# Seven-product form for the first two batches' outputs, queries of batch 2 transposed on TensorE, and tail stores by quarter block

## The chip, the cores and the metric

One core of one Trainium2 chip. The time is that of the whole kernel on the device, in microseconds (us), median of its runs. The traces give a span, first to last instruction, which is some 1.8 us shorter. In the profile PE is TensorE's matmuls, PEld its weight loads, DVE VectorE, ACT ScalarE, POOL GpSimd, SP SyncE. A line such as `67.48 0.50 PE L293 ... [1.83 <-DVE t_bkv L271]` is: start, duration, engine, source line, operation, output and input, and in brackets the engine's idle time just before it and what ended it.

## The reference

Eight batches of 8 heads, 576 tokens and 64 channels go through an attention over 32 memory slots, then a SwiGLU block with 512 channels and a hidden width of 1536. The kernel takes and gives float32, and computes in bfloat16.

```python
a = softmax over tokens of phi                     # phi: 8 x 8 x 576 x 32
k_m = einsum('bhsm,bhsd->bhmd', a, k); v_m = the same with v
attn = softmax(q @ k_m.T / sqrt(64)) @ v_m         # 8 x 8 x 576 x 64
x = attn.transpose(0, 2, 1, 3).reshape(4608, 512)
g = x @ w_gate; val = x @ w_val                    # 512 -> 1536
out = (g * sigmoid(g) * val) @ w_out               # 1536 -> 512
```

## The kernel before

The kernel runs batches 0 and 1 together, up to about 54 us, then a batch at a time. Output products of a batch wait in a `backlog` and are fed to TensorE between the steps of the next one.

For batches 2 to 7 the product with `w_out` is made of seven products of half blocks instead of eight (a Winograd form). It needs block sums of the hidden activations (`t_S`: four operations for each of three chunks, two of the chunks on GpSimd and one on VectorE) and of the weights (`t_T`: four for each chunk, once, on VectorE). Batches 0 and 1 take the plain product, which needs no sums:

```python
def out_units(b, u, eng):          # plain: 12 matmuls of 512 columns for 128 tokens
    ...
        nc.tensor.matmul(mine["p"], lhsT=hts[b, jf // 4][:, jf % 4, 128 * u:128 * (u + 1)],
                         rhs=WO[jf], start=(jf == 0), stop=(jf == NJF - 1))
    ...
def weight_sums(c):                # VectorE, both inputs in SBUF
    ...
    subtract(v, t[:, 0], B12, B11);  subtract(v, t[:, 1], B22, t[:, 0])
    subtract(v, t[:, 2], B22, B12);  subtract(v, t[:, 3], B21, t[:, 1])
    Ts[c] = t
def chunk_done(b, c):              # when chunk c of batch b's hidden activations is complete
    ...
    if b < FAST:                   # FAST = 2: no sums for batches 0 and 1
        ends()
        return
    eng = nc.vector if c + 1 == NCH else nc.gpsimd
    ...
    eng.tensor_tensor(out=t[:, 0], in0=A21, in1=A22, op=ALU.add)
    subtract(eng, t[:, 1], t[:, 0], A11)
    subtract(eng, t[:, 2], A11, A21)
    subtract(eng, t[:, 3], A12, t[:, 1])
    ...
```

Each product takes a bank of PSUM, from a list of eight in the order in which they were given back. A product is summed in its bank, VectorE adds it to a stored earlier one, and the bank is free. In the list of seven, "s", "a" and "c" are banks, and several products go to the same one:

```python
first = product("s", A(0, 0), W_(0, lo), "p1") + product("a", A(1, 0), W_(1, lo), "c11")
five = product("c", Sx(0), T(0), "p5")
six = product("s", Sx(1), T(1), "q6")
three = product("c", Sx(3), W_(1, hi), "c12")
seven = product("s", Sx(2), T(2), "c22")
four = product("s", A(1, 1), T(3), "c21")
return first + five + six + three + seven + four, ops
```

`p1`, `p5`, `q6` are ScalarE's copies of a bank; `c11` to `c21` are the additions that complete an output quarter (VectorE). Queries of batches 2 and 3 share one buffer (`Q_SLOT = (0, 1, 0, 0, ...)`); those of batch 2 are transposed by the DMA.

The softmax here doesn't subtract the row's maximum and nothing guards it: scores larger than these inputs give would overflow.

## Time and profile before

| | before |
|---|---|
| time, median (first runs: lowest to highest) | 238.47 us (238.07 to 242.48) |
| span of the profiled execution, granted clock | 237.7 us, 0.998 |
| PE busy | 225.7 us (95%) |
| batch 2's first scores, batch 3's first scores (first matmul of L400) | 67.03, 96.89 us |
| PE waits between 54 and 100 us | 1.7 for `t_qT`, 0.5 small |
| from PE's last matmul to the end | 5.1 us |

The two rows of scores are the marks to go by: between them and after them the work is the same, so a change shows as a shift of the marks.

### The profile page before, as it was taken

The page shows a single profiled execution, that of the slowest core. Times are in us where ns is not written, and L with a number is a line of the kernel's source. Part 1 is how long each engine was busy: PE and PEld are TensorE (multiplying, and loading weights), DVE is VectorE, ACT ScalarE, POOL GpSimd, SP SyncE. Part 2 cuts the span into 40 slices and gives each one's busy share as a digit, 9 for nine tenths or more (in the row PEclk, how much of TensorE's full clock was granted, in tenths as well). Part 3 has the DMA queues.
Part 4 walks back from the last instruction along what each step waited for, and adds up shares of the span by engine and source line. Part 5 has one row for each costly group of instructions (what it writes and reads, how often), then busy time and mean ns, then how long its engine had stood idle before and what let it go on. Part 6 is the DMA issues. An engine that isn't in the chain of part 4 may idle for free.

```text
span 237.7 us, 7051 instructions
## 1 busy us (share of the span) xinstructions
PE 225.7 (95%) x2745; PEld 163.0 (69%) x2751; DVE 183.0 (77%) x410; ACT 169.5 (71%) x361; POOL 110.5 (47%) x149
## 2 busy tenths in 40 slices
PE   7988899999999999799999999999999999999991
PEld 2554467775544767587778777877788778878880
DVE  4247699995578888698789878988799879987621
ACT  2768889986067769687898779968897788677310
POOL 8523432000072297344992499167926492039400
PEclk9999999999999999999999999999999999999999
DMA  6999999998889999999169954999396621122206
GB/s 212 204 205 206 199 207 209 242 235 182 112 176 208 254 190 95 203 242 209 47 120 201 256 110 99 201 290 121 94 167 145 116 89 24 39 53 88 47 8 190
DMA packets 44592, 37.41 MB, mean 157 GB/s; under 512 B 17680, under 2 KB 39696, under 8 KB 44560
## 3 DMA queue, kind: packets, MB, share of 16 engines
q0 software_dynamic: 21424, 22.42, 56.2%
q1 hardware_dynamic: 22160, 13.38, 26.5%
q10 hardware_dynamic: 976, 1.18, 1.5%
q8 instruction: 21, 0.34, 0.6%
q14 instruction: 11, 0.09, 0.2%
HBM read 42.47 MB, written 9.44 MB: 218 GB/s over the span
## 4 chain that ended last, share of the span: by engine, by line
PE 65%; DMA 20%; DVE 7%; ACT 2%; issue 2%; POOL 2%; DVEq 0%; POOLq 0%
PE p_g L514 16%; PE p_v L514 15%; PE p_os L713 9%; PE p_oo L633 8%; DMA t_qT<-t_q 8%; DMA W<-in_moe_w_gate_dram 7%; PE p_u L471 4%; PE p_oc L713 4%; DMA t_kv<-in_k_dram 3%; PE p_oo L661 3%; PE p_oa L713 2%; DMA t_kT<-t_bkv 2%; ACT t_U L491 2%; PE p_kv L235 2%; DVE t_lz L443 1%
## 5 line engine op out<-in xcount | busy, mean ns | idle before, releaser
L537 DVE TENSOR_TENSOR t_h<-t_sg,p_v 128x288 bf16<-128x288 bf16 x192 | 83.7, 452 | 14.9 <-PE p_v L514 9.6
L514 PEld LDWEIGHTS <-t_U 128*128 128x128 bf16 x768 | 73.8, 98 | 22.2 <-issue 2.6
L531 ACT ACTIVATE t_sg<-p_g 128x288 bf16<-128x288 f32 x192 | 75.1, 420 | 18.8 <-PE p_g L514 11.8
L514 PE MATMUL p_g<-t_A,t_U 128*128 128x288 bf16 x384 | 77.1, 286 | 0.1
L514 PE MATMUL p_v<-t_A,t_U 128*128 128x288 bf16 x384 | 76.9, 286 | 0.0
L491 ACT CAST t_U<-p_u 128x512 bf16<-128x512 f32 x53 | 28.0, 607 | 8.4 <-PE p_u L471 8.4
L713 PEld LDWEIGHTS <-t_S 128*128 128x128 bf16 x288 | 28.2, 98 | 3.3
L598 POOL TENSOR_TENSOR t_S<-t_h 128x512 bf16<-128x512 bf16 x12 | 13.9, 1154 | 35.6 <-DVE t_h L537 35.6
L713 PEld LDWEIGHTS <-t_h 128*128 128x128 bf16 x216 | 20.4, 98 | 6.2 <-issue 3.2
L633 PE MATMUL p_oo<-WO,t_h 128*128 128x512 bf16 x90 | 21.6, 379 | 0.6 <-issue 0.5
L115 POOL DMA_DIRECT2D t_q<-in_q_dram x6 | 4.8, 798 | 32.2 <-DMA t_qT<-t_q 30.7
L713 PE MATMUL p_os<-t_T,t_S 128*128 128x256 bf16 x144 | 17.7, 273 | 0.0
L633 PEld LDWEIGHTS <-t_h 128*128 128x128 bf16 x96 | 9.0, 98 | 10.6 <-issue 1.1
L471 PE MATMUL p_u<-W,t_kT 64*32 64x512 bf16 (+1 forms) x416 | 16.0, 363 | 0.3 <-DMA W<-in_moe_w_gate_dram 0.2
L661 PE MATMUL p_oo<-WO,t_x 128*128 128x256 bf16 x96 | 14.5, 273 | 0.0
L560 POOL TENSOR_TENSOR t_S<-t_S,t_h 128x512 bf16<-128x512 bf16 x12 | 13.8, 1154 | 0.9
L560 POOL TENSOR_TENSOR t_S<-t_h,t_S 128x512 bf16<-128x512 bf16 x12 | 13.9, 1155 | 0.0
L560 POOL TENSOR_TENSOR t_S<-t_h 128x512 bf16<-128x512 bf16 x12 | 13.9, 1155 | 0.0
L836 PE MATMUL p_warm<-bones 128*128 128x512 bf16 (+2 forms) x43 | 12.1, 406 | 1.7 <-DVE bones L859 1.7
L495 DVE CAST t_U<-p_u 128x512 bf16<-128x512 f32 x19 | 12.4, 683 | 1.5 <-PE p_u L471 1.5
L451 DVE TENSOR_TENSOR t_A<-t_E,t_lz 128x576 bf16<-128x576 bf16 x16 | 12.1, 757 | 1.2 <-DVE t_lz L443 0.5
L411 ACT ACTIVATE t_E<-p_g 128x288 bf16<-128x288 f32 x12 | 5.0, 414 | 10.4 <-PE p_v L400 10.4
(93 smaller groups left out, 311.5 us busy)
## 6 DMA issues: line engine op xcount, KB each, us to landing
t_kv<-in_k_dram POOLq DMA_DIRECT2D x8, 576.0 KB, 8.1
t_kv<-in_v_dram POOLq DMA_DIRECT2D x8, 576.0 KB, 14.1
out_dram<-t_o SPq DMA_DIRECT2D x23, 192.0 KB, 2.9
t_phi<-in_phi_dram POOLq DMA_DIRECT2D x6, 576.0 KB, 16.3
t_q<-in_q_dram POOLq DMA_DIRECT2D x6, 576.0 KB, 10.8
out_dram<-t_o SPq DMA_DIRECT2D x36, 64.0 KB, 2.6
out_dram<-t_o SPq DMA_DIRECT2D x15, 128.0 KB, 3.8
WO<-in_moe_w_out_dram POOLq DMA_DIRECT2D x3, 512.0 KB, 18.8
```

The source lines that it names most:

```text
L451: nc.vector.tensor_tensor(out=a, in0=es.pop((b, g)), in1=lzs.pop((b, g)), op=ALU.mult)
L471: nc.tensor.matmul(p[g][32 * i:32 * i + 32, o:o + n], lhsT=kTs[b][64 * g:64 * g + 64, 2, 32 * i:32 * i + 32], rhs=w_part(w, c, i, g, halve ...
L491: nc.scalar.copy(out=t, in_=p)
L495: nc.vector.tensor_copy(out=t, in_=p)
L514: nc.tensor.matmul(p[:, 0:HALF], lhsT=Us[b, c, g][:, o // 2, which, 128 * (o % 2):128 * (o % 2 + 1)], rhs=atts[b, g][:, r], start=(g == 0) ...
L531: nc.scalar.activation(out=sg, in_=gate[:, 0:HALF], func=AF.Silu)
L537: nc.vector.tensor_tensor(out=dst, in0=sg, in1=val[:, 0:HALF], op=ALU.mult)
L560: eng.tensor_tensor(out=out, in0=x, in1=y, op=ALU.subtract)
L598: eng.tensor_tensor(out=t[:, 0], in0=A21, in1=A22, op=ALU.add)
L633: nc.tensor.matmul(mine["p"], lhsT=hts[b, jf // 4][:, jf % 4, 128 * u:128 * (u + 1)], rhs=WO[jf], start=(jf == 0), stop=(jf == NJF - 1),)
L661: nc.tensor.matmul(mine["p"], lhsT=xs[pair][:, jf].rearrange("p a t -> p (a t)"), rhs=WO[jf][:, cols], start=(jf == 0), stop=(jf == NJF - 1),)
L713: nc.tensor.matmul(mine[home][:, u], lhsT=lhs(c, m, u), rhs=rhs(c, m), start=fresh and u == 0, stop=(k == 5), skip_group_check=u == 1 or n ...
```

## The change

The intent: TensorE is full, so take matmul time from it (the seven-product form for batches 0 and 1 too), let batch 3's queries be loaded early, and send the last outputs sooner. The diff, cut to its core:

```diff
-    Q_SLOT = (0, 1, 0, 0, 1, 0, 1, 0)
+    Q_SLOT = (0, 1, 0, 1, 0, 1, 0, 1)
@@ chunk_done
-        if b < FAST:
-            ends()
-            return
...
+        if b == 0 and c > 0:
+            late.append(lambda: sums(nc.vector if end else nc.gpsimd))
+        else:
+            sums(nc.vector if end else nc.gpsimd)
...
+        if (b, c) in beside_sums:
+            beside_sums[b, c]()       # loads of batch 3, behind GpSimd's sums
@@ c11, c22, c12, c21
+            if box.get("end"):
+                both("o1", 0, lo)     # store a quarter as soon as it is summed
@@ start
-    load_q(2)
-    load_q(3)
+    for g in range(NG):
+        load_q_group(2, g)
@@ batch 2
-    backlog = out_list(0) + out_list(1) + out_rest(0, 0)
+    backlog = []
...
-            load_qT(2)
             phi_exp(2)
-            run(take(16))
-            weight_sums(0)
-            run(take(12))
-            run(kv_items(2)[:1] + take(6) + kv_items(2)[1:] + take(7))
-            weight_sums(1)
-            run(take(11))
+            (one, ops1), (zero, ops0) = products(1, ()), products(0, ())
+            kv, q2 = kv_items(2), q_items(2, "aava")
+            run(one[:6])
+            for c in range(NCH):
+                weight_sums(c)
+            run(one[6:12] + zero[:6] + kv[:1] + q2[:2])
+            run(one[12:18] + kv[1:] + q2[2:])
+            mark = ...                # GpSimd waits here for batch 2's keys
+            run_late()                # sums of batch 0's chunks 1 (GpSimd) and 2 (VectorE)
+            run(one[18:36])
+            backlog = zero[6:] + one[36:] + out_rest(0, 0)
...
-                ([lambda: load_qT(3)], 12, 12),
@@ end
+    box["end"] = True
     run(take(6))
     ops["c11"]()
-    box["end"] = True
```

Batch 3's query transpose is issued right after batch 2's scores instead.

More of the change, by code (lines that the diff above doesn't have):

```diff
@@ L480, in u_round @@
                 if (b, c, g) not in Us:
-                    Us[b, c, g] = upool.tile([128, 2, 2, HC], BF16, tag=f"U{c}{g}", name="t_U")
+                    u_buffer(b, c, f"U{c}")
                 if len(which) == 1:
@@ L548, in gv_slot, with u_buffer @@
         flush_mul(n)
-    def u_buffers(b):
-        for c in range(NCH):
-            t = upool.tile([128, NG, 2, 2, HC], BF16, tag=f"S{c}", name="t_U")
-            for g in range(NG):
-                Us[b, c, g] = t[:, g]
+    def u_buffer(b, c, tag):
+        t = upool.tile([128, NG, 2, 2, HC], BF16, tag=tag, name="t_U")
+        for g in range(NG):
+            Us[b, c, g] = t[:, g]
     xs, Ss, late = {}, {}, []
@@ L589, in ends, with sums @@
             )
-        if b < FAST:
-            ends()
-            return
-        eng = nc.vector if c + 1 == NCH else nc.gpsimd
-        t = upool.tile([128, 4, 2, 256], BF16, tag=f"S{c}", name="t_S")
+        t = upool.tile([128, 4, 2, 256], BF16, tag=f"U{c}" if b == 1 else f"S{c}", name="t_S")
         Ss[b, c] = t
         A11, A12, A21, A22 = blocks(b, c)
-        eng.tensor_tensor(out=t[:, 0], in0=A21, in1=A22, op=ALU.add)
-        subtract(eng, t[:, 1], t[:, 0], A11)
-        subtract(eng, t[:, 2], A11, A21)
-        subtract(eng, t[:, 3], A12, t[:, 1])
-        if c + 1 < NCH:
-            ends()
-        else:
-            late.append(ends)
+        def sums(eng):
+            eng.tensor_tensor(out=t[:, 0], in0=A21, in1=A22, op=ALU.add)
+            subtract(eng, t[:, 1], t[:, 0], A11)
+            subtract(eng, t[:, 2], A11, A21)
+            subtract(eng, t[:, 3], A12, t[:, 1])
+        end = c + 1 == NCH
+        if b == 0 and c > 0:
+            late.append(lambda: sums(nc.vector if end else nc.gpsimd))
+        else:
+            sums(nc.vector if end else nc.gpsimd)
+        if end and b > 1:
+            late.append(ends)
+        else:
+            ends()
+        if (b, c) in beside_sums:
+            beside_sums[b, c]()
+    beside_sums = {
+        (0, 0): lambda: load_q(3), (1, 0): lambda: load_k(3), (1, 1): lambda: load_v(3)
+    }
     def token_segments(b, t0, count):
@@ L623, in store @@
             eng.dma_start(out=out_r[bb, jj, pp:pp + m, cols], in_=t_o[row + r0:row + r0 + m])
-    def out_units(b, u, eng):
-        mine = {}
-        def unit(jf):
-            def run():
-                if jf == 0:
-                    mine["p"] = bank([128, DM], FP32, "p_oo")
-                nc.tensor.matmul(
-                    mine["p"],
-                    lhsT=hts[b, jf // 4][:, jf % 4, 128 * u:128 * (u + 1)],
-                    rhs=WO[jf],
-                    start=(jf == 0),
-                    stop=(jf == NJF - 1),
-                )
-                if jf == NJF - 1:
-                    t_o = work.tile([128, DM], FP32, tag="to", name="t_o")
-                    copy(eng, t_o, mine["p"])
-                    done(mine["p"])
-                    store(t_o, b, 128 * u, 128)
-            return run
-        return [unit(jf) for jf in range(NJF)]
     def out_rest(pair, half):
@@ L743, in add, with both @@
                 done(mine[home])
+        def both(name, t0, cols):
+            for u in range(2):
+                store(mine[name][:, u, cols], b, t0 + 128 * u, 128, cols=cols)
         def c11():
@@ L751, in c22 @@
             add(t[:, :, hi], "s", "p5")
+            if box.get("end"):
+                both("o2", 256, hi)
         def c12():
@@ L755, in c12 @@
             add(t[:, :, hi], "c", "q6", True)
-            for u in range(2):
-                store(t[:, u], b, 128 * u, 128)
+            both("o1", 0, hi if box.get("end") else slice(0, DM))
         def c21():
@@ L762, in c21 @@
             done(mine["s"])
-            for u in range(2):
-                store(t[:, u], b, 256 + 128 * u, 128)
+            both("o2", 256, lo if box.get("end") else slice(0, DM))
         ops = dict(
@@ L779, in products @@
         return first + five + six + three + seven + four, ops
-    FAST = 2
-    def out_list(b):
-        res = []
-        for u in range(4):
-            res += out_units(b, u, "a" if u < 2 else "v")
-        return res
     def q_items(b, evac):
@@ L880 @@
     load_phi(3, nc.gpsimd)
-    load_q(2)
-    load_q(3)
-    u_buffers(1)
+    for g in range(NG):
+        load_q_group(2, g)
+    for c in range(NCH):
+        u_buffer(1, c, f"S{c}")
     warm(104)
@@ L947, in take @@
         return part
-    KV = {b: 7 for b in range(3, B - 1)}
+    KV = 7
     def loads(b):
@@ L969 @@
         if b == 2:
-            load_qT(2)
             phi_exp(2)
-            run(take(16))
-            weight_sums(0)
-            run(take(12))
-            run(kv_items(2)[:1] + take(6) + kv_items(2)[1:] + take(7))
-            weight_sums(1)
-            run(take(11))
+            (one, ops1), (zero, ops0) = products(1, ()), products(0, ())
+            kv, q2 = kv_items(2), q_items(2, "aava")
+            run(one[:6])
+            for c in range(NCH):
+                weight_sums(c)
+            run(one[6:12] + zero[:6] + kv[:1] + q2[:2])
+            run(one[12:18] + kv[1:] + q2[2:])
+            mark = att.tile([1, 1], BF16, tag="mark", bufs=1, name="t_mark")
+            nc.gpsimd.tensor_copy(out=mark, in_=kTs[2][0:1, 0, 0:1])
+            run_late()
+            run(one[18:36])
+            backlog = zero[6:] + one[36:] + out_rest(0, 0)
         else:
@@ L980 @@
             run(take(6))
-            loads(b)
+        loads(b)
         for g in range(NG):
@@ L987 @@
         if b == 2:
-            load_k(3)
-            load_v(3)
-            load_q(4)
-            load_phi(4, nc.gpsimd)
-        else:
-            run(take(6))
+            load_qT(3)
+        run(take(6))
         z_inv_v(b, 0)
@@ L997 @@
             ops["c11"]()
-            run(take(6))
+        run(take(6))
         if not last:
@@ L1002 @@
         norm(b, 1)
-        if b > 2:
-            run(take(6))
+        run(take(6))
         run_late()
@@ L1007 @@
         if b == 2:
-            run(take(24))
+            run(take(6))
             u_three(2)
-            weight_sums(2)
         run(take(12))
@@ L1014 @@
         outs = [lambda: run(take(1)) for _ in range(len(backlog) - beside)]
-        streams = [(g, 0, 24), (outs, 4 if b > 2 else 0, 24)]
+        streams = [(g, 0, 24), (outs, 4, 24)]
         if last:
             streams += [([u_item(b, 2)], 5, 6)]
-        if b == 2:
-            streams += [
-                ([lambda: load_qT(3)], 12, 12),
-                ([lambda: (load_k(4), load_v(4))], 12, 12),
-                (kv_items(3, lambda: (u_item(2, 2, "aava")(), run(take(2)))), 12, 16),
-                ([lambda: (run(take(2)), u_three(3), run(take(3)))], 17, 18),
-            ]
-        elif not last:
-            load_qT(b + 1)
-            phi_sum(b + 1)
-            streams += [
-                (kv_items(b + 1, lambda: (u_item(b, 2, "aava")(), run(take(2)))), KV[b], KV[b] + 4),
+        if not last:
+            if b == 2:
+                streams += [([lambda: (load_k(4), load_v(4))], 12, 12)]
+            else:
+                load_qT(b + 1)
+                phi_sum(b + 1)
+            streams += [
+                (kv_items(b + 1, lambda: (u_item(b, 2, "aava")(), run(take(2)))), KV, KV + 4),
                 ([lambda: (run(take(2)), u_three(b + 1), run(take(3)))], 19, 20),
```

## The prediction

> **What bounds the kernel now.** I read the page's first two parts, then the windows by stage, the timelines of PE, POOL, DVE and the DMA queue, and the chain of waits.
>
> ```profile
> PE 225.7 (95%) x2745; PEld 163.0 (69%) x2751; DVE 183.0 (77%) x410; ACT 169.5 (71%) x361; POOL 110.5 (47%) x149
> ```
>
> PE is busy for 95% of the span, so time leaves this kernel only if PE gets less work, if one of its few holes closes, or if the ends shorten. The windows say where the holes are (length, then busy time of PE, PEld, DVE, ACT, POOL, then clock, DMA share, GB/s):
>
> ```profile
> 54.40:67.00 12.60, 12.39 (x136) 6.03 (x136) 5.91 (x18) 3.77 (x5) 0.00 (x0) 1.00 0.82 143
> 67.00:97.00 30.00, 27.89 (x341) 17.96 (x352) 25.08 (x54) 22.21 (x47) 17.11 (x23) 1.00 1.23 178
> 97.00:122.20 25.20, 25.20 (x338) 19.91 (x338) 21.05 (x45) 20.88 (x45) 16.48 (x22) 1.00 0.78 171
> 232.60:237.70 5.10, 0.00 (x0) 0.00 (x0) 0.42 (x1) 0.00 (x0) 0.00 (x0) 0.92 0.57 175
> ```
>
> A later batch takes 25.2 us and PE fills all of it. Batch 2 (54.4 to 97.0) leaves PE idle 2.3 us, and after PE's last matmul 5.1 us go to the final stores. The one large hole, with its cause:
>
> ```profile
> 40.00 0.79 POOL L115 DMA_DIRECT2D t_q<-in_q_dram  x1 [1.52 <-DMA W<-in_moe_w_val_dram]
> 67.06 0.77 POOL L115 DMA_DIRECT2D t_q<-in_q_dram  x1 [26.27 <-DMA t_qT<-t_q]
> ...
> 77.79 8.71 SPq L121 DMA_TRANSPOSE t_qT<-t_q  x1
> ...
> 96.89 0.28 PE L400 MATMUL p_g<-t_qT,t_kT 64*32 64x288 bf16 x1 [1.67 <-DMA t_qT<-t_q]
> ```
>
> Queries of batches 2 and 3 share one buffer. So POOL sits 26.3 us until the DMA transpose of batch 2 has read it, batch 3's queries are loaded late, their transpose is issued at 77.8 among the other loads and takes 19.1 us to land, and PE waits 1.67 us for it.
>
> The cost of the output products, from the chain (start, length):
>
> ```profile
> 63.22 3.88 PE p_oo L633 x18
> ...
> 102.89 1.31 PE p_os L713 x12
> ```
>
> An old 512-column matmul is 3.88/18 = 0.2156 us; a 256-column one of the seven-product form is 1.31/12 = 0.109 us. (The page counts 90 of the 96 old ones, so some records are missing and I use counts from the code.)
>
> **What the Trainium skill says.** (1) "TensorE: Matmul & The Clock Gate", section "Wait — 56ns, not 53.3ns?": a warm matmul costs N/2.4 GHz plus about 2.5 ns, so 215.8 ns for 512 columns and 109.2 for 256; the two durations above agree. (2) "VectorE: DVE Perf Modes", section "The three transpose paths": a DMA transpose is several times slower than TensorE's, whose result lands in PSUM and needs a copy. This trace agrees: 6.4 to 19.1 us to landing for a DMA transpose of one batch's queries, while 12 of the start's TensorE transposes pass in about 0.5 us (11.89 to 12.39) and a copy takes 0.45 us. (3) "GPSIMD Engine Reference", section "1. Specifications": the SBUF interface is shared with VectorE, with contention for DVE instructions that have two SBUF inputs. The trace shows it faintly: a POOL copy that lasts 0.40 us lasts 0.66 beside DVE's block sums at 197.7, and DVE's sums last 0.50 to 0.51 instead of 0.42 beside POOL's copies at 221.5. DVE's gate products at L537 (one SBUF input) stay at 0.42 to 0.45 us with or without POOL's sums. (4) "DMA: Bandwidth & Descriptors", section "Anatomy of one DMA — SWDGE (gpsimd) path": a transfer has a fixed cost of about 2 us, mostly the write receipt. A lone late store here (at 223.8) lands in 1.9 to 2.2 us.
>
> **The change part by part.**
>
> *PE work.* Removed: 96 matmuls of 512 columns, 96 x 0.2156 = 20.7 us. Added: 2 batches x 7 products x 12 matmuls = 168 x 0.109 = 18.35 us. Net -2.35 us, all on the path because PE is full here. Added: 24 transposes of batch 2's queries, 2 x 0.5 = +1.0 us. Net -1.35 us.
>
> *The hole.* With slots that alternate and batch 2's queries transposed on TensorE, batch 3's load no longer waits for a DMA transpose. It follows the first POOL sums, near 48 us; its transpose is issued right after batch 2's scores (near 68) and even with 19 us to landing is done 6 us before it is needed. -1.67 us.
> Sum if nothing new waits: -3.0. Adding up PE's new sequence from 54.6 by the same durations puts batch 3's scores at 93.4 instead of 96.89, which is -3.5 (the small holes of the old sequence go too). I take -3.2.
>
> *The new wait.* The old stage opened with about 48 matmuls that needed nothing from DVE. The new one needs, at once, all weight sums and the block sums of batch 1. DVE in program order after its last gate product at 55.2:
>
> ```profile
> 55.20 0.42 DVE L560 TENSOR_TENSOR t_T<-WO 128x512 bf16<-128x512 bf16 x1
> 55.65 0.42 DVE L560 TENSOR_TENSOR t_T<-WO,t_T 128x512 bf16<-128x512 bf16 x1
> 55.99 0.42 DVE L560 TENSOR_TENSOR t_T<-WO 128x512 bf16<-128x512 bf16 x1
> 56.33 0.42 DVE L560 TENSOR_TENSOR t_T<-WO,t_T 128x512 bf16<-128x512 bf16 x1
> ...
> 61.83 0.99 DVE L271 TENSOR_SCALAR t_bkv<-p_kv,t_rS 128x128 bf16<-128x128 f32 x4
> ```
>
> Four such operations pass in 1.45 us. There are 4 groups (block sums of the last chunk, three of weights): 5.8 us to 61.0; an output sum 0.65, a reciprocal 0.2, the four scalings 0.99: 62.8. PE's independent work from 54.6: three products 3.93, the key and value sums 0.95, 12 transposes 0.5, the first sum product 1.31: 61.3. The next thing on PE is the transpose of those scalings. So PE waits about 1.6 us at best. POOL, by its queue (second query load at 42.3 when an earlier load frees its place, then 4 x 1.15 us for each chunk's sums, copies and loads between), does the sums of batch 1's middle chunk from about 55 to 59.5, beside those very DVE operations, both with two SBUF inputs. Either DVE stretches (12 x 0.08 = 1.0 us) or POOL is held and its sums come late. I add 0.6. Wait: +2.2 us.
>
> *The tail.* DMA share by microsecond (the last columns):
>
> ```profile
> 232.00:233.00 1.00, 0.58 (x6) 0.28 (x3) 0.38 (x2) 0.00 (x0) 0.00 (x0) 1.00 0.90 285
> 233.00:234.00 1.00, 0.00 (x0) 0.00 (x0) 0.05 (x1) 0.00 (x0) 0.00 (x0) 1.00 0.96 285
> 235.00:236.00 1.00, 0.00 (x0) 0.00 (x0) 0.00 (x0) 0.00 (x0) 0.00 (x0) 1.00 0.64 223
> ```
>
> Two blocks of 512 KB and the last 128 KB, 1.15 MB, at 285 GB/s are 4.1 us, which is the stretch from 231.6 to 235.7: the tail is a transfer, not one latency. Storing each quarter when it is summed moves 512 KB ahead of 230.7. The rest then ends near 234.7, and the last store lands in about 2.1 us instead of 3.1. -1.0 us. PE's work before it does not change.
>
> *Sum.* -3.2 + 2.2 - 1.0 = -2.0 us, thus 238.47 - 2.0 = 236.5. From batch 3 on nothing moves, 25.2 us a batch.
>
> **The rivals.** (A) DVE and POOL take the whole gain of batch 2: if POOL's sums of the middle chunk cannot run at all beside DVE's chain, they end near 65.5, three products wait for them in turn, and the stall is 3 to 4 us. For it: the copy at 0.66 us above. Against: POOL may be ahead of my count. It makes 237.5 to 238.3. (B) PE's wait is covered, because POOL's and DVE's sums run faster than I count: the full 3.2 + 1.0, thus 234.3. For it: the order of the new stage puts a batch 0 product and query transposes before the first sum product. Against: the same DVE rows, which add to 62.8 without any contention. (C) POOL's sums in the stage of batches 0 and 1 slow DVE's gate products, where DVE is busy 27.1 of 28.9 us, and DVE becomes that stage's bound: 10% slower would be 29.8, +0.9 us and 237.4. Against: those products do not stretch beside POOL in later batches. (D) The quarter stores have 1 KB rows and twice as many issues, so the tail gains nothing: 237.5.
>
> **Range and chances.** The stall carries most of the doubt (1.6 best by count, 4 worst, 0 if I misread the order): +-1.3; the tail +-0.5. Range 234.7 to 237.9. Faster by over 2% means below 233.7: no stall, a full tail and something more, 0.06. Slower by over 2% (above 243.2) needs a surprise such as C at full size: 0.02. Within 2%: 0.92.
>
> **What would show it.** Right: 168 matmuls in place of the 512-column ones and PE busy down by about 1.4 us; no wait for t_qT at batch 3's scores; a new PE idle of 1.6 to 3 us before the transpose of t_bkv or in the first sum product, near 60 to 63, ended by DVE or POOL; batch 3's scores near 95.5; later batches at 25.2; from PE's last matmul to the end near 4.1 us instead of 5.1. Wrong: no idle over 0.5 us in that place (B), t_S of POOL as the releaser with over 3 us (A), the stage of batches 0 and 1 longer than 28.9 us (C), or a tail still of 5 us (D).

## The result, and the profile after

The changed kernel took 247.75 us (247.6 to 248.35, 4 runs), against 238.47: a ratio of 1.040, 95% interval 1.038 to 1.043. It is slower by 4%, where within 2% had been given 0.92. (A ratio here and below is the mean time of one kernel's fast runs over that of the other's in the same rounds, so not quite the ratio of the medians quoted.) Executions over 1.5% slower than the fastest of the same kernel are left out of the means.

| | before | after |
|---|---|---|
| span, granted clock | 237.7, 0.998 | 246.6, 0.979 |
| PE busy, VectorE busy | 225.7, 183.0 | 229.9, 195.9 |
| batch 2's, batch 3's first scores | 67.03, 96.89 | 74.99, 106.1 |
| last matmul to the end | 5.1 | 4.5 |

Nearly all of the loss arises between 54 and 106 us: 8.0 us before batch 2's scores and 1.3 more before batch 3's. From batch 3's first scores to batch 7's it is 101.6 us instead of 101.3 (batch 3 itself takes 25.7 instead of 25.2). The view of waits of PE of the changed kernel, 54 to 100 us (total, times, longest):

```profile
PE p_oc L697 <- DVE t_T L559: 2.8, 3, 1.4
PE p_u L471 <- DVE t_o L725: 1.9, 1, 1.9
PE p_T L293 <- DVE t_bkv L271: 1.8, 1, 1.8
PE p_os L697 <- DVE t_o L725: 0.8, 1, 0.8
```

The wait for `t_qT` is gone, as forecast. In its place are waits for VectorE: 4.6 us for weight sums and the scaled keys, and 2.7 us for output additions, of which the forecast knew nothing. VectorE's timeline of the same kernel says why it is late:

```profile
57.89 1.37 DVE L559 TENSOR_TENSOR t_S<-t_h 128x512 bf16<-128x512 bf16 x1
59.19 1.37 DVE L559 TENSOR_TENSOR t_S<-t_h,t_S 128x512 bf16<-128x512 bf16 x1
...
65.30 0.42 DVE L559 TENSOR_TENSOR t_T<-WO,t_T 128x512 bf16<-128x512 bf16 x1
...
66.43 0.99 DVE L271 TENSOR_SCALAR t_bkv<-p_kv,t_rS 128x128 bf16<-128x128 f32 x4
...
72.51 1.37 DVE L559 TENSOR_TENSOR t_S<-t_h,t_S 128x512 bf16<-128x512 bf16 x1
```

The same size of sum takes 0.42 us at 65.3 and 1.37 us at 57.9, 59.2 and 72.5. At those times GpSimd makes its own two-input sums (POOL's timeline):

```profile
58.94 1.33 POOL L559 TENSOR_TENSOR t_S<-t_h,t_S 128x512 bf16<-128x512 bf16 x1
...
72.27 1.33 POOL L559 TENSOR_TENSOR t_S<-t_h,t_S 128x512 bf16<-128x512 bf16 x1
```

VectorE's sum lasts as long as GpSimd's. There are two such pairs of chunks, 55.5 to 60.5 and 68.9 to 73.9. GpSimd's own sums lengthen only from 1.15 to 1.33 us, and no wait for them is listed: VectorE is the one held up. The scalings end at 67.4 instead of the 62.8 of the forecast. Then comes a second thing, in the windows of the changed kernel (length, busy time of PE, PEld, DVE, ACT, POOL, then granted clock, DMA share, GB/s) and in PE's timeline:

```profile
62.00:64.00 2.00, 0.83 (x4) 0.55 (x4) 1.97 (x6) 0.00 (x0) 0.50 (x1) 0.76 1.20 202
...
66.00:68.00 2.00, 0.52 (x6) 0.53 (x7) 1.38 (x6) 1.60 (x4) 0.00 (x0) 0.50 0.44 74
...
70.00:72.00 2.00, 2.00 (x12) 1.43 (x10) 1.97 (x3) 0.46 (x1) 2.00 (x2) 0.50 0.00 0
```

```profile
68.74 2.76 PE L697 MATMUL p_os<-t_T,t_S 128*128 128x256 bf16 x12
71.29 2.45 PE L697 MATMUL p_oc<-WO,t_S 128*128 128x256 bf16 x12
```

From 63 to 73 us, in and after this stall, the granted clock is 0.50 (whether the stall causes it is tested in e9), and two products of twelve matmuls take 2.55 and 2.29 us from start to start instead of 1.31. In the trace that is PE busy time, not a wait: PE busy rose by 4.2 us though the work shrank.

So there were three suspects: contention of VectorE and GpSimd, the half clock, and the waits for output additions later in batch 2. The experiments take them one at a time.

### The profile page after: what moved, and what is told of

The parts are those of the page before. It is cut to its first block, busy times and chain, and to the rows that moved or that the text cites.

```text
span 246.6 us, 7300 instructions
## 1 busy us (share of the span) xinstructions
PE 229.9 (93%) x2847; PEld 173.2 (70%) x2847; DVE 195.9 (79%) x421; ACT 172.6 (70%) x368; POOL 130.9 (53%) x167
## 4 chain that ended last, share of the span: by engine, by line
PE 64%; DVE 16%; DMA 7%; POOL 5%; issue 3%; ACT 2%; ACTq 0%; DVEq 0%; POOLq 0%
PE p_g L514 17%; PE p_v L514 16%; PE p_os L697 12%; DMA t_kv<-in_v_dram 7%; PE p_oc L697 5%; PE p_u L471 4%; PE p_oo L645 4%; DVE t_h L537 3%; DVE t_S L559 3%; PE p_oa L697 2%; POOL t_es L217 2%; DVE t_T L559 2%; DVE t_o L725 2%; DVE t_lz L443 2%; DVE t_z L434 2%
## 5 line engine op out<-in xcount | busy, mean ns | idle before, releaser
L514 PEld LDWEIGHTS <-t_U 128*128 128x128 bf16 x768 | 73.8, 98 | 21.2 <-issue 2.6
L697 PEld LDWEIGHTS <-t_S 128*128 128x128 bf16 x384 | 38.9, 102 | 9.4 <-issue 3.8
L595 POOL TENSOR_TENSOR t_S<-t_h 128x512 bf16<-128x512 bf16 x16 | 18.5, 1155 | 46.2 <-DVE t_h L537 46.2
L697 PEld LDWEIGHTS <-t_h 128*128 128x128 bf16 x288 | 27.3, 98 | 8.9 <-issue 5.0
L697 PE MATMUL p_os<-t_T,t_S 128*128 128x256 bf16 x192 | 24.9, 282 | 0.1
L559 POOL TENSOR_TENSOR t_S<-t_S,t_h 128x512 bf16<-128x512 bf16 x16 | 18.6, 1162 | 1.3
L559 POOL TENSOR_TENSOR t_S<-t_h,t_S 128x512 bf16<-128x512 bf16 x16 | 18.8, 1178 | 0.0
L559 POOL TENSOR_TENSOR t_S<-t_h 128x512 bf16<-128x512 bf16 x16 | 18.8, 1176 | 0.0
L697 PE MATMUL p_os<-t_T,t_h 128*128 128x256 bf16 x96 | 15.9, 273 | 0.8 <-DVE t_o L725 0.8
L697 PE MATMUL p_oc<-t_T,t_S 128*128 128x256 bf16 x96 | 12.9, 284 | 2.8 <-DVE t_T L559 2.8
L697 PE MATMUL p_oc<-WO,t_S 128*128 128x256 bf16 x96 | 12.8, 287 | 0.0
L697 PE MATMUL p_oa<-WO,t_h 128*128 128x256 bf16 x96 | 11.8, 273 | 0.2 <-ACT t_E L411 0.2
## 6 DMA issues: line engine op xcount, KB each, us to landing
t_q<-in_q_dram POOLq DMA_DIRECT2D x5, 576.0 KB, 10.2
```

The lines of the kernel that those rows point to most:

```text
L514: nc.tensor.matmul(p[:, 0:HALF], lhsT=Us[b, c, g][:, o // 2, which, 128 * (o % 2):128 * (o % 2 + 1)], rhs=atts[b, g][:, r], start=(g == 0) ...
L559: eng.tensor_tensor(out=out, in0=x, in1=y, op=ALU.subtract)
L697: nc.tensor.matmul(mine[home][:, u], lhsT=lhs(c, m, u), rhs=rhs(c, m), start=fresh and u == 0, stop=(k == 5), skip_group_check=u == 1 or n ...
```

## The experiments

Twelve experiments ran, three or five rounds each but for e4. All gave the reference's result but e7, which is wrong. All times are of fast runs but e4's, and medians are taken over these.

### e1: the tail stores alone

Before, with only the `both(...)` stores and `box["end"] = True` two lines earlier, as in the diff above.

> The kernel before with the quarter-block stores alone. In the changed kernel the stretch from the last matmul of TensorE to the end is 4.46 us where it was 5.1, and TensorE waits 0.15 us more for a copy on ScalarE that stands behind the new store issues. If the tail part stands alone, this is 0.5 us faster than before (ratio 0.998). If the forecast of 1.0 us was right and something else in the changed kernel ate half of it, 0.996. If 1 KB rows cost as much as the earlier start gives, 1.000.

Measured: 237.10 us, ratio 0.995 (0.992 to 0.997). The forecast's tail term, -1.0, was -1.2; in the trace the stretch from PE's last matmul to the end is 4.3 us instead of 5.1 (forecast: 4.1). This part pays, and the loss lies elsewhere.

### e2: the queries alone

```diff
-    Q_SLOT = (0, 1, 0, 0, 1, 0, 1, 0)
+    Q_SLOT = (0, 1, 0, 1, 0, 1, 0, 1)
-            load_qT(2)
+            kv, q2 = kv_items(2), q_items(2, "aava")
-            run(kv_items(2)[:1] + take(6) + kv_items(2)[1:] + take(7))
+            run(kv[:1] + q2[:2] + take(6) + kv[1:] + q2[2:] + take(7))
+            load_qT(3)                # after batch 2's scores
```

> The kernel before with only the second part: alternating query slots, batch 2's queries transposed on TensorE, batch 3's queries loaded at once. Theory of the prediction: minus 1.67 us of waiting for the transposed queries, plus 1.0 us of transposes on TensorE, so 0.3 to 0.9 us faster (ratio 0.996 to 0.999). If this part is what made the changed kernel slow (its transposes wait, or early loads disturb), it is 1 us or more slower.

Measured: 239.14 us, ratio 1.0025 (1.001 to 1.004): slower by 0.6 us, though its trace has no wait for `t_qT`. The wait of 1.67 us belonged to one execution. In e1's trace, of a kernel that is the one before in this place, it was shorter:

```profile
PE p_g L400 <- DMA t_qT<-t_q: 0.9, 1, 0.9
```

In e12's trace, of the same kernel as e1, none is listed. Against e12, both marks of e2 stand 1.0 us later (68.18 and 96.21 instead of 67.19 and 95.23): the transposes' 1.0 us shows in full where the old kernel had no hole to close.

### e3: GpSimd's sums ahead of its loads

The changed kernel, in which GpSimd issues the loads of batch 2's queries and batch 3's `phi` behind its first sums, so that its sums come earlier than VectorE's.

```diff
-        (0, 0): lambda: load_q(3), (1, 0): lambda: load_k(3), (1, 1): lambda: load_v(3)
+        (0, 0): lambda: (load_phi(3, nc.gpsimd), load_q_group(2, 0), load_q_group(2, 1)),
+        (1, 0): lambda: (load_q(3), load_k(3)), (1, 1): lambda: load_v(3),
```

> The changed kernel with GpSimd's order turned: block sums of batches 0 and 1 go ahead of the loads that were queued before them, so that the sums of batch 1's middle chunk end near 54.6 us, before VectorE begins its block and weight sums at 55.5. Port theory (a VectorE sum with two SBUF inputs lasts as long as the GpSimd sum beside it): VectorE's four block sums take 0.42 us each instead of 1.2 to 1.4, its chain ends near 63 instead of 67.4, TensorE's stall shrinks from 4.6 to about 1.7 us, its clock stays at 1.0, so two products take 1.31 us instead of 2.6 and 2.3: 6 to 7 us faster than the changed kernel, near 241 us. Rival (VectorE's sums are slow there for another reason, or the stall is in TensorE's own order): the same sums still take over 1 us and the time stays near 247.

Measured: 244.24 us (one of four runs was slow), ratio 1.026 (1.023 to 1.028), 3.5 us under the changed kernel where 6 to 7 had been expected. VectorE's first four sums take 0.50 to 0.73 us, and batch 2's scores come at 70.69. Still there: a wait of 2.24 us for the scaled keys, the half clock after it, the second pair of sums and both later waits.

### e4: needless sums beside the kernel before

The kernel before, with nine needless two-input sums on GpSimd from 56 us on. The load of batch 3's queries moves behind them.

```diff
-    load_q(3)
...
+    for x, y in ((A21, A22), (A11, A21), (A12, A22)) * 3:
+        nc.gpsimd.tensor_tensor(out=t_x, in0=x, in1=y, op=ALU.add)
+    load_q(3)
```

> The disputed cost by itself: the kernel before, with nine needless GpSimd sums of two SBUF inputs (written to a scratch tile) from about 55.6 us on, beside VectorE's weight sums of chunks 0 and 1, which nothing there waits for. Port theory: those weight sums last 1.1 to 1.4 us each instead of 0.42 while GpSimd works, and VectorE's operations on PSUM in the same stretch (scalings 0.28 to 0.35, output copies 0.69) stay as they were. Rival of a mild contention as I forecast: 0.5 us each.

Measured: 248.34 us in one run of unknown state. VectorE's weight sums, of unchanged code, just as GpSimd starts, and POOL's timeline:

```profile
55.30 0.42 DVE L560 TENSOR_TENSOR t_T<-WO 128x512 bf16<-128x512 bf16 x1
...
57.48 1.37 DVE L560 TENSOR_TENSOR t_T<-WO,t_T 128x512 bf16<-128x512 bf16 x1
```

```profile
55.95 11.42 POOL L943 TENSOR_TENSOR t_scratch<-t_h 128x512 bf16<-128x512 bf16 x9
```

The slowing is thus made by GpSimd's sums and not by the changed order. VectorE's operations that read PSUM keep their length there (four scalings 0.99 us as before). Most of the 10 us of this kernel are something else: GpSimd's loads, put behind the sums, and with them the query transpose, come late, and PE waits 2.06 us for a load of values and 5.11 us for `t_qT`. Its time proves nothing, the two durations do.

### e5: work to keep the clock, in a bank that was not free

Needless products (`warm`) in the four gaps of the changed kernel.

> The changed kernel, with needless matrix products (12, 20, 6 and 28 units of 128 columns, some 0.7, 1.1, 0.3 and 1.5 us at full clock) put into the four waits of TensorE between 60 and 69 us. They change no wait: VectorE's chain still ends near 67.4 us. Theory that the stall costs twice, by itself (4.6 us) and by the half clock granted afterwards: the granted clock stays at 1.0 from 66 to 73 us, the twelve instructions of the sixth product take 1.3 us again instead of 2.55, the following ones 1.3 instead of 2.25, batch 2's scores come near 72.3 us instead of 75.0 and the whole is 2.5 to 3 us shorter than the changed kernel, about 245.0 us. Rival, that the clock falls for some other reason (power, the transposes themselves) or that the half clock is hidden behind VectorE's and GpSimd's second pair of sums anyway: the clock is 0.5 all the same, or it is 1.0 and the time stays within 0.7 us of 247.7.

Measured: 254.02 us, ratio 1.065. The edit was at fault: the needless products took a bank that VectorE frees at the end of its chain, PE stood 4.53 us for it, and the clock fell to 0.50 all the same. It is mended in e9.

### e6: the order of the backlog

```diff
-            backlog = zero[6:] + one[36:] + out_rest(0, 0)
+            backlog = one[36:] + zero[6:] + out_rest(0, 0)
```

> The changed kernel with one line altered: the fourth product of batch 1 stands at the head of the backlog instead of behind batch 0's products. Theory that batch 2's two new waits of TensorE (1.89 us ahead of the first gate product, 0.78 us ahead of the fourth product) come from the order in which products and their bank releases fall: with the order of the later batches both waits go, and the time falls by 2 to 2.7 us to about 245.3 us, while the stall near 61 to 67 us and the half clock stay as they are. Rival, that VectorE's own backlog after its contended sums makes TensorE wait there in any order: the two waits stay or move to another product, and the time is within 0.7 us of 247.7.

Measured: 245.07 us, ratio 1.027 (1.024 to 1.031), 2.7 us under the changed kernel. PE's waits, 54 to 100 us:

```profile
PE p_oc L697 <- DVE t_T L559: 3.2, 3, 1.4
PE p_T L293 <- DVE t_bkv L271: 2.2, 1, 2.2
PE p_os L697 <- DVE t_o L725: 0.2, 1, 0.2
```

The 1.9 and the 0.8 us are gone, and nothing else improved. So the order made these two waits. How, I read from the code and did not test further: the fourth product of batch 1, put behind all of batch 0, had shifted the backlog by one product against the later batches: a product met its own bank before VectorE had read it (0.8 us), and `u_three` wanted a bank that an addition had not given back (1.9 us).

### e7: GpSimd's sums replaced by copies (wrong result)

```diff
+            if eng is nc.gpsimd and b < 2:
+                for n, x in enumerate((A21, A11, A22, A12)):
+                    eng.tensor_copy(out=t[:, n], in_=x)
+                return
```

> Wrong result on purpose: the changed kernel in which GpSimd's four two-input sums of each chunk of batches 0 and 1 are four copies of one input, at the same places and in the same number. If two-input work of both engines holds each other up, VectorE's sums beside them fall from 1.2 to 1.4 us back to 0.42 to 0.7, its chain ends near 63 us instead of 67.4, the idle of TensorE falls from 4.6 to under 2 us, the clock does not fall to a half, and the time is 5 to 7 us under the changed kernel (241 to 243 us). If instead any work of GpSimd on the same memory slows VectorE as much, the sums stay above 1.0 us and the time stays above 246 us.

Measured: 241.5 us, ratio 1.013 (1.010 to 1.017), 6.25 us under the changed kernel. VectorE's and GpSimd's timelines:

```profile
56.42 0.41 DVE L559 TENSOR_TENSOR t_S<-t_h 128x512 bf16<-128x512 bf16 x1
...
64.33 0.79 DVE L599 TENSOR_TENSOR t_S<-t_h 128x512 bf16<-128x512 bf16 x1
```

```profile
64.24 2.85 POOL L597 COPY t_S<-t_h 128x512 bf16<-128x512 bf16 x4
```

The chain ends at 63.3, PE waits 1.70 us for the scaled keys (the forecast's "about 1.6 us at best"), the clock stays at 1.00 over it, and batch 2's scores come at 68.03. The two waits that e6 removes, 1.9 and 0.8 us, are still listed, so e6's gain and e7's are separate. (In this profiled execution, at 242.72 us the slowest of the four, the clock is 0.50 from 77.0 to some 80.4 us, after the wait of 1.89 us; in the changed kernel's trace the same wait, which ends at 83.9, is not followed by it.) One caution: GpSimd's copies are shorter (0.71 us each), so those of batch 1 are over before VectorE's chain starts. Only the second pair overlaps, and there VectorE's sums take 0.71 to 0.82 us, again about the length of GpSimd's operation. So copies hold VectorE up as well, for as long as they last; two inputs on GpSimd's side are not needed for it.

### e8: a rearrangement that failed

e3 and e6 together; VectorE scales batch 2's keys before the later weight sums; both late chunks of batch 0 are summed on GpSimd, after the weight sums.

```diff
-            run(one[6:12] + zero[:6] + kv[:1] + q2[:2])
-            run(one[12:18] + kv[1:] + q2[2:])
+            weight_sums(0)
+            run(one[6:12] + kv[:1])
+            weight_sums(1)
+            weight_sums(2)
+            run(zero[:6] + q2[:2] + kv[1:] + q2[2:] + one[12:18])
+            ops1["c11"]()
```

> The changed kernel rearranged: GpSimd's sums ahead of its loads of later batches as in the third experiment; VectorE scales batch 2's keys before the later weight sums, so that TensorE's transposes need not wait for the whole chain; chunks 1 and 2 of batch 0 both summed on GpSimd, after VectorE's weight sums are done; the fourth product of batch 1 at the head of the backlog. If the three causes (contended sums, half clock, order of products) are all of the loss, the two-input sums hardly overlap, TensorE waits less than 1 us before batch 2's scores, which come near 66 to 67 us, its clock stays above 0.95, and the time is 234 to 236 us, under both kernels and under the tail stores alone (237.1). If something else in the change costs (transposes, queues, banks), it stays above 238.

Measured: 243.14 us, ratio 1.020 (1.017 to 1.022), far over the 234 to 236 expected. ScalarE's and PE's timelines:

```profile
64.89 0.58 ACT L727 COPY t_p<-p_os 128x512 f32<-128x512 f32 x1 [7.25 <-DVE t_o L732]
65.38 1.73 ACT L388 COPY t_qT<-p_q 128x576 bf16<-128x576 bf16 x3
```

```profile
66.07 2.72 PE L704 MATMUL p_oc<-t_T,t_S 128*128 128x256 bf16 x12 [4.51 <-POOL t_S L600]
```

The profile names GpSimd as the releaser of PE, but the sums that this product needs were done before 58 us. What also ends just then, near 66 us, is the first of ScalarE's three query copies; by the order in which banks are given back, worked out from the code, the product takes the bank that this copy reads. The copies stood behind a copy into `t_p`, which has one buffer, held until an addition that I had put last in VectorE's order. The inferred name was that of an operation which happened to end at the same time; with the copies moved, among other things (e10), the wait is 0.75 us, for another bank.

### e9: the clock kept, in the product's own bank

```diff
+            warm(12)
+            run(one[12:14])
+            idle_work(11)         # matmuls of zeros, added to the fifth product
+            run(one[14:16])
+            idle_work(3)
+            run(one[16:17])
+            idle_work(15)
+            run(one[17:18] + kv[1:] + q2[2:])
```

> The fifth experiment mended: there the needless products took a bank that VectorE's addition of batch 1's first block frees only at the end of its chain, so TensorE stood 4.5 us for the bank. Here the first gap is filled with 12 units of 128 columns as before, and the later ones with 11, 3 and 15 products of 256 columns with zeros, added to the fifth product's own bank (0.109 us each, together about 3.2 us of the 3.7 us that TensorE stands there), the last of them ahead of that product's last chunk. VectorE's chain is as in the changed kernel, so the stall has the same end, near 67.5 us. Theory: the granted clock stays at 1.0, the sixth and third product take 1.3 us again instead of 2.55 and 2.25, batch 2's scores come near 72.3 us, the time is 2.5 to 3 us under the changed kernel (about 245 us). Rival: the clock falls all the same, or the gain is lost again at VectorE's contended second pair of sums, and the time is within 0.7 us of 247.7.

Measured: 248.06 us (247.29 to 250.32), ratio 1.035 (1.027 to 1.042); the kernel before was uneven (238.13 to 241.66 in its fast runs), so the time says only that no 2.5 us were gained. A window and a line of PE's timeline:

```profile
66.00:68.00 2.00, 1.39 (x19) 1.05 (x18) 1.53 (x7) 1.52 (x3) 0.00 (x0) 1.00 0.46 78
```

```profile
74.46 0.41 PE L471 MATMUL p_u<-W,t_kT 64*32 64x512 bf16 x7 [1.56 <-DVE t_o L726]
```

With PE kept busy the clock stays at 1.00, the two products take 1.31 us again, and batch 2's scores come at 72.27, 2.7 us sooner. Then PE waits 1.56 us for a bank that VectorE frees only after its second contended pair of sums, which ends at 73.8 as before; the product after that wait starts 1.0 us sooner than in the changed kernel (74.80 instead of 75.83). Batch 3's scores come at 105.1 instead of 106.1. So theory and rival were each half right: the idle does cost the clock, and most of that cost was hidden behind VectorE, which was late anyway. Adding 2.7 us for the clock to the contention would have counted the same time twice.

### e10: the rearrangement mended

e8, with the weight sums by element over all chunks, the addition for batch 1 earlier, and ScalarE's copy for batch 0 after the query copies.

```diff
+            w = [weight_sums(c) for c in range(NCH)]      # returns the four steps
+            run(one[:6] + [x[0] for x in w] + one[6:12] + kv[:1])
+            run([x[1] for x in w])
+            ops1["c11"]()
+            run(zero[:6] + q2[:2] + kv[1:] + q2[2:])
+            ops0["p1"]()
+            run([x[n] for n in (2, 3) for x in w] + one[12:18])
```

> The eighth experiment with its fault mended: there ScalarE's copies of batch 2's queries stood behind its copy of batch 0's first product, whose one buffer was freed by VectorE's addition for batch 1, put last; the bank of the fifth product hung on those copies (4.5 us, and the half clock after it). Now VectorE makes the weight sums by element over all three chunks (first, second, then after the scalings of keys and the addition for batch 1 the third and fourth), and ScalarE's copy of batch 0's first product comes after the copies of queries. Expected: TensorE waits under 0.5 us between 55 and 66 us, full clock throughout, batch 2's scores near 66.3 us, batch 3's near 94.3 us, the time 235 to 236.5 us, under the kernel before (238.4) and under the tail stores alone (237.1). Above 238 us something else in the change would have to cost.

Measured: 236.91 us, ratio 0.988 (0.982 to 0.993), with the uneven kernel before. Batch 2's scores at 67.17, batch 3's at 96.4 instead of the 94.3 expected. VectorE's and GpSimd's timelines have the reason:

```profile
70.22 3.98 DVE L451 TENSOR_TENSOR t_A<-t_E,t_lz 128x576 bf16<-128x576 bf16 x1
```

```profile
69.10 2.26 POOL L559 TENSOR_TENSOR t_S<-t_h,t_S 128x512 bf16<-128x512 bf16 x2
71.33 2.26 POOL L559 TENSOR_TENSOR t_S<-t_h 128x512 bf16<-128x512 bf16 x2
```

This scaling of scores has two inputs in SBUF and takes 0.76 us elsewhere. Here it stands in the middle of GpSimd's eight sums of batch 0, and ends only after the last of them. Beside the same eight sums VectorE's operations with one input in SBUF keep their 0.78 us (the reduction at 68.30, the transpose at 69.41), and its additions that read PSUM their 0.69 us (at 66.04 and 67.28).

### e11: batch 0's late sums on VectorE as well

e10, with batch 0's late sums on VectorE too (four before batch 2's scores, four behind the first scaling), and the fifth product's bank taken before the addition for batch 1.

```diff
-            late.append(parts(nc.gpsimd))
+            late.append(parts(nc.vector))
...
+            run(zero[:6] + q2[:2] + kv[1:] + q2[2:] + one[12:13])
             ops1["c11"]()
...
+            run(sums0[:4] + one[18:36])
...
+        if b == 2:
+            run(sums0[4:])        # after norm(2, 0)
```

> The tenth experiment with the last contention taken out: there the scaling of batch 2's first scores on VectorE (two inputs in SBUF) stood beside GpSimd's sums of batch 0 and took 3.98 us instead of 0.76, which held TensorE up by about 1 us (0.69 and some shorter waits). Now VectorE makes the sums of batch 0's chunks 1 and 2 itself, alone: eight of some 0.42 us, four of them ahead of batch 2's scores and four behind the first scaling; GpSimd makes none there. And the fifth product takes its bank before VectorE's addition for batch 1, which cost 0.75 us. If the contention is the point, VectorE does more and is still sooner: its eight sums take under 4 us together, the scaling 0.76, TensorE waits under 0.4 us from 55 to 95 us, batch 3's scores come near 94.2 us and the time is about 235.2 us, 1 us or more under the tail stores alone. If VectorE was short of time as such, TensorE waits at batch 2's gate products instead and nothing is gained.

Measured: 236.19 us (236.1 to 236.43, 4 runs), ratio 0.991 (0.989 to 0.992). VectorE's timeline and PE's only listed wait between 54 and 100 us:

```profile
64.54 0.76 DVE L602 TENSOR_TENSOR t_S<-t_h 128x512 bf16<-128x512 bf16 x2
...
69.53 0.76 DVE L451 TENSOR_TENSOR t_A<-t_E,t_lz 128x576 bf16<-128x576 bf16 x1
```

```profile
PE p_os L706 <- DVE t_o L734: 0.2, 1, 0.2
```

Batch 1's sums at 55.6 us still stand beside GpSimd's last sum and its copies and take 0.50 to 0.75 us; the long pairs are gone. VectorE took over eight operations from GpSimd and is sooner done: eight sums in 2.9 us, where GpSimd needed 9 us (e10) and VectorE lost 3.2 us in one operation beside them. Batch 3's scores come at 94.4. The time is 1 us above the 235.2 expected.

### e12: the tail alone, beside e11

> The tail stores alone once more, to have them beside the kernel above on the same chip in the same rounds: 0.995 of the kernel before as in the first experiment (237.1 us where the kernel before takes 238.4). The kernel above should be under it by 1 us or more if the sums, the queries on TensorE and the tail each pay; equal to it if only the tail does.

Measured: 237.15 us, ratio 0.993 (0.991 to 0.996), in the same rounds as e11. The intervals of the two ratios overlap a little, the runs do not: e11's slowest of 4 took 236.43 us, e12's fastest of 10 236.81. So e11 is the fastest kernel, by about 1 us under the tail alone and 2.4 us under the kernel before (238.55 in that call). PE busy is 226.2 us in e12 and 225.0 in e11.

## Why the prediction was wrong

**The failed step is "The new wait: +2.2 us"; PE waited 4.6 us there** (2.8 for weight sums, 1.8 for the scaled keys). The mechanism was forecast: the part without contention, "about 1.6 us at best", was right (1.70 us in e7), and so was the time at which GpSimd's sums run beside VectorE's ("about 55 to 59.5"; 55.2 to 60.3). What was mis-sized is the contention, "12 x 0.08 = 1.0 us ... I add 0.6". VectorE's sixteen sums took 10.2 us (55.47 to 65.63), against 5.9 in e7: 4.2 us more, for the first meeting alone. The 0.08 us came from VectorE's sums beside a GpSimd *copy* at one place of the trace (0.50 instead of 0.42); I saw the sign of a contention there and took its size from there too. Beside GpSimd's long sums VectorE's take up to 1.37 us, 0.95 more, some ten times the 0.08; e4 shows the same for unchanged code.

Rival A named the right pair of engines and the wrong loser: it had GpSimd's sums held up to 65.5 us and PE waiting for them. They ended at 60.3, and VectorE's chain at 67.4. Neither it nor the forecast saw that a *second* pair, the late chunks of batch 0, meets in the same way at 69 to 74 us. Both pairs together, with the half clock that followed, cost 6.25 us by e7, not 0.6.

**Two consequences were not in the forecast.** The backlog's order cost 2.7 us (e6): I counted the sequence of matmuls, not when each bank is given back. The half clock costs 2.7 us at batch 2's scores, but most of it is hidden (e9: 1.0 us at batch 3's scores).

**PE work, -1.35: about right.** 225.0 us in e11 against 226.2 in e12 is -1.2 us, in a kernel without the half clock.

**The hole, -1.67: wrong as a gain.** It was read from an execution that took 1 us more than the median one. In e12's trace it is not there, and e2 gained nothing from closing it. The two terms together, -3.2, are worth about -1.0 where nothing waits (e11 against e12).

**Tail, -1.0: right** (-1.2 in e1). The Trainium skill's 2 us that the prediction cites stand in a section on transfers issued by GpSimd; the stores are issued by SyncE, so only the 1.9 to 2.2 us of the trace bear on them. **Rival C: false**, the stage of batches 0 and 1 kept its length (TensorE's output products start at 54.59 us, before at 54.43). **Rival B**, a covered wait with 234.3 us, is what e11 sets up; it gave 236.2, for the hole was not to be had.

**The sum.** The forecast missed by 11.25 us. Contention beyond the 0.6: 5.65. Order: 2.7. Hole and PE work: 2.2 less gained than forecast. Tail: 0.2 more. Together 10.35; some 0.9 us I cannot assign (about 0.3 of it lies after batch 3's first scores). e11, with the contended pairs, the order and the half clock all gone, has nothing of the loss left. The parts come from different kernels and need not add up exactly.

## What to carry to other kernels

Work moved to GpSimd is not free for VectorE operations with two inputs in SBUF: look for a place in the trace where just those two kinds of operation overlap, and take its duration, not that of a milder pair; if there is none, measure it by itself before counting on it. Where the overlap can't be avoided in time, the faster engine may as well do both. When a new order of work is planned, follow the buffers and banks through it as well as the operations, and before counting a hole as gain, see whether it is in more than one execution.

## What the Trainium skill lacked or had wrong

- "GPSIMD Engine Reference", section "1. Specifications", names contention with VectorE's instructions of two SBUF inputs and is right; no size stands there. The skill as a whole does not lack the rule: "SBUF — State Buffer", section "SBUF: two separate sides", says which of the two operations is held and for how long, and I did not use it. The sizes here: VectorE's 128x512 bfloat16 sum went from 0.42 to 1.37 us beside GpSimd's sums, which themselves went from 1.15 to 1.33. Beside GpSimd's plain copies of 0.71 us it was 0.71 to 0.82 us (e7). In e10 a scaling of 128x576 went from 0.76 to 3.98 us: it began with one of GpSimd's sums, at 70.2, and outlasted three of them.
- "TensorE: Matmul & The Clock Gate", section "What's actually happening", gives the half clock after at least one idle window of about 3.4 us. Here a window that was not wholly idle was enough: in e3 the clock fell to 0.50 at 65 us after a wait of 2.24 us, the longest there and shorter than such a window, with PE busy for about 1.2 of the 3.4 us before the fall; it stayed at 0.50 for about 3.4 us, which agrees with the page's window. In e7 a wait of 1.70 us left it at 1.00. A wait of 1.89 us was followed by 0.50 in e7's trace and not in the changed kernel's. That section names no share of busy time that keeps the clock up.
- No page that I used warns that the releaser which a profile names is only the last event that fits in time: in e8 it named GpSimd's sums for 4.5 us that a bank behind ScalarE's copies had cost.
